# A linear-attention plus spectral-mixing kernel: f32 x is no longer kept from the attention stage but formed again during the weight stream, and nine modes of weights are prefetched instead of seven

## The chip, the cores and the metric

The kernel runs on one core of a Trainium2 chip. The metric is the device time of one execution in microseconds (us). The profile of a kernel comes from one execution; its span (first to last instruction) is about 1.8 us shorter than the time of the same execution. In the profile PE is TensorE (PEld its weight loads), DVE is VectorE, ACT is ScalarE, POOL is GpSimd and SP is SyncE. The kernel keeps its tiles in SBUF and the results of its matmuls in PSUM, two memories of the core.

## The reference, cut to what matters

```python
# attention: q, k, v are (B=8, H=8, S=576, Dh=64)
q_p, k_p = phi(q), phi(k)                       # phi(x) = elu(x) + 1
kv  = einsum('bhsd,bhse->bhde', k_p, v)         # 64 x 64 for each head
z   = sum(k_p, axis=2)
x   = einsum('bhsd,bhde->bhse', q_p, kv) / (einsum('bhsd,bhd->bhs', q_p, z) + 1e-6)
x   = x.transpose(0, 2, 1, 3).reshape(B, S, 512)
# spectral mixing: 64 modes, each with its own 512 x 512 complex weight
X = rfft(x, axis=1)[:, :64]
Yr = Xr @ w_r - Xi @ w_i ;  Yi = Xr @ w_i + Xi @ w_r      # per mode
u = x + irfft(Y, n=S, axis=1)
out = u + maximum(u @ w_ch, 0)
```

The weights w_r and w_i are 64 x 512 x 512 f32 each, 134 MB together; q, k and v are 28 MB. The kernel lets the DMA cast everything to 16 bits on the way into SBUF. One **half mode** below is w_r or w_i of one mode: 1 MB in memory, 512 KB in SBUF.

## The kernel before

The kernel has three stages. Attention runs over eight batches and produces f32 x (kept in SBUF to the end) and its transform `xt_c`. Then the weight stream multiplies mode after mode, with the products x @ w_ch of 36 tiles of x spread between the modes. The last stage transforms back, adds and writes the output.

Attention needs the transform of **all** batches before mode 0 can be multiplied, so weights that arrive during attention have to be stored. Two pools do that: `wpre` (4 buffers, used once, inside the attention scope) holds modes 0 and 1, and `wpool` (10 buffers, recycled for the whole stream) holds modes 2 to 6.

```python
x_main = [xpool.tile([128, NJJ, D], F32, ...) for b in range(B)]     # 64 KB a partition
x_tail = [xpool.tile([128, D], F32, ...) for i in range(B // 2)]     #  8 KB a partition
W_KEEP = 10                     # recycled half-mode buffers
W_PRE = 4                       # half-mode buffers used once
n_pre = W_PRE // 2

for b in range(B):
    for nm, src in (("q", q), ("k", k), ("v", v)):
        t = sA.tile([...], F16, tag="raw", bufs=5, ...)      # one ring for q, k and v
        nc.gpsimd.dma_start(out=t, in_=...)
    # ... weights for mode b/2 - 1; phi(q), phi(k); k^T v; q^T into qT (bufs=1) ...
    for jj in range(NJJ + 1):
        # num = qT^T @ [kv | z]  (8 small matmuls)
        nc.vector.reciprocal(out=rden[orow], in_=nv[:, :, :, 64])
        dst = xtl[orow, :] if tail else xm[:, jj, :]                 # f32 x, kept
        nc.vector.tensor_tensor(out=dst, in0=nv[..., 0:64], in1=rden..., op=ALU.mult)
        if tail: nc.scalar.copy(out=x16t[orow, :], in_=dst)
        else:    nc.gpsimd.tensor_copy(out=x16[:, jj, :], in_=dst)   # f16 copy for the transform
    # ... xf = transform of x16 (20 matmuls); xt_c <- xf (VectorE and ScalarE) ...

def mode_product(kk, ...):
    wr, wi = w_get(kk)          # loads a later mode into the buffers that are freed
    # P = 4 matmuls with wr, 4 with wi; P -> f16; 4 small matmuls into yt_ps
# ... modes 0..63, after mode 4 also: channel_product(t): x16w <- x_of(t), transposes, eps = xT^T @ wch, E0[t] <- eps
```

A load can only be issued when its buffer is free, and all loads of q, k, v and w are issued by POOL, in order. The engines execute their own instructions in the order that the compiler's scheduler gave them.

Of the kernel before, what the change touches and what calls it, by code (L numbers as in the profile page):

```python
# [16 lines left out]
NJ = 9  # L17
# [3 lines left out]
def _dft_consts(S: int, NM: int):  # L21
# [5 lines left out]
    for jj in range(4):  # L27
        for j2 in range(2):
            s = NJ * p + 2 * jj + j2
            ang = 2.0 * np.pi * np.outer(s, m) / S  # L30
            fwd[j2 * 64 : j2 * 64 + 64, jj, :NM] = np.cos(ang)
            fwd[j2 * 64 : j2 * 64 + 64, jj, NM:] = -np.sin(ang)
            s_cols[jj * 128 + j2 * 64 + p] = s
# [20 lines left out]
def kernel(  # L54
# [46 lines left out]
    x_main = [  # L101
        xpool.tile([128, NJJ, D], F32, tag="x_main", bufs=B, name=f"x_main{b}") for b in range(B)
    ]
    x_tail = [
        xpool.tile([128, D], F32, tag="x_tail", bufs=B // 2, name=f"x_tail{i}")
        for i in range(B // 2)
    ]
# [9 lines left out]
    W_KEEP = 10  # L117

    def w_load(kk: int, pool, tag: str, bufs: int):
        got = []  # L120
        for name, src in (("wr", moe_w_r), ("wi", moe_w_i)):
            w = pool.tile([128, NDC, D], BF16, tag=tag, bufs=bufs, name=f"{name}{kk}")
            nc.gpsimd.dma_start(out=w, in_=src[kk].rearrange("(p dc) e -> p dc e", dc=NDC))
            got.append(w)
        return got
# [4 lines left out]
    sA_ctx = ExitStack()  # L130
    sA = sA_ctx.enter_context(tc.tile_pool(name="sA", bufs=1))
    psA = sA_ctx.enter_context(tc.tile_pool(name="psA", bufs=1, space=bass.MemoryType.PSUM))
    W_PRE = 4
    wpre = sA_ctx.enter_context(tc.tile_pool(name="wpre", bufs=1))
    n_pre = W_PRE // 2

    vpad = [sA.tile([128, NHP, NJ, 66], F16, tag="vpad", bufs=1, name=f"vpad{i}") for i in range(1)]
    for t in vpad:
        nc.vector.memset(t[:, :, :, 64:66], 1.0)

    for b in range(B):
        raw = {}
        for nm, src in (("q", q), ("k", k), ("v", v)):
            t = sA.tile([128, NHP, NJ * Dh], F16, tag="raw", bufs=5, name=f"{nm}16_{b}")
            nc.gpsimd.dma_start(
                out=t,
                in_=src[b].rearrange("h s d -> (h s) d").rearrange(
                    "(hp r j) d -> r hp (j d)", r=128, j=NJ
                ),
            )  # L150
            raw[nm] = t
        if b % 2 == 0 and b > 0:
            kk = b // 2 - 1
            if kk < n_pre:
                w_in[kk] = w_load(kk, wpre, "wp", W_PRE)
            else:
                w_in[kk] = w_load(kk, wpool, "w", W_KEEP)

# [15 lines left out]
        vp = vpad[0]  # L174
# [18 lines left out]
        kv_sb = sA.tile([128, 2, 2, 65], F16, tag="kv_sb", bufs=2, name=f"kvs{b}")  # L193
# [9 lines left out]
        qT = sA.tile([128, 2, 2, NJ * NP], F16, tag="qT", bufs=1, name=f"qT{b}")  # L203
        qp = phi["q"]
        for hpp in range(2):
            qT_ps = psA.tile([128, NJ, 2, NP], F16, tag="big", bufs=3, name=f"qTp{b}_{hpp}")
            for j in range(NJ):
                nc.tensor.transpose(
                    qT_ps[:, j].rearrange("p t r -> p (t r)"),
                    qp[:, hpp, j].rearrange("p o d -> p (o d)"),  # L210
                    id16,
                )
# [5 lines left out]
        xm, xtl = x_main[b], x_tail[b // 2]  # L218
# [3 lines left out]
        for jj in range(NJJ + 1):  # L222
# [3 lines left out]
            for hpp in range(2):  # L226
                for h2 in range(2):
                    for hpo in range(2):
                        rows = slice(hpo * 64, hpo * 64 + 64)
                        c0 = (hpp * 2 + h2) * 65  # L230
                        cols = slice(512, 576) if tail else slice(jj * 128, jj * 128 + 128)
                        nc.tensor.matmul(  # L232
                            num[orow, hpo, c0 : c0 + 65],
                            qT[rows, hpp, h2, cols],
                            kv_sb[rows, hpp, h2, :],
                        )
            nv = num[orow, :, 0:260].rearrange("p o (c n) -> p o c n", c=4)
            rden = sA.tile([128, 2, 4], F32, tag="rden", bufs=3, name=f"rd{b}_{jj}")
            nc.vector.reciprocal(out=rden[orow], in_=nv[:, :, :, 64])
            dst = xtl[orow, :] if tail else xm[:, jj, :]  # L240
# [3 lines left out]
                in1=rden[orow].unsqueeze(3).broadcast_to([64 if tail else 128, 2, 4, Dh]),  # L244
                op=ALU.mult,
            )
            if tail:
                nc.scalar.copy(out=x16t[orow, :], in_=dst)
            else:
                nc.gpsimd.tensor_copy(out=x16[:, jj, :], in_=dst)  # L250
# [14 lines left out]
    n_in = len(w_in)  # L265


    def w_get(kk: int):
        if kk not in w_in:
            w_in[kk] = w_load(kk, wpool, "w", W_KEEP)  # L270
        return w_in.pop(kk)

    def mode_product(kk: int, ps, stage, yt_ps):

        wr, wi = w_get(kk)
        P = ps.tile([128, D], F32, tag="P", bufs=2, name=f"P{kk}")
# [21 lines left out]


    nc.gpsimd.dma_start(out=wch16, in_=moe_w_ch.rearrange("(c p) j -> p c j", p=128))  # L300
    while n_in < n_pre + W_KEEP // 2:
        w_in[n_in] = w_load(n_in, wpool, "w", W_KEEP)
        n_in += 1
    first = {}
    for kk in range(n_pre):
        first[kk] = w_in[kk]

    ystage0 = ctx.enter_context(tc.tile_pool(name="ystage", bufs=1, side="right"))
    def open_w_psum():
        return tc.alloc_tile_pool(name="psW", bufs=1, space=bass.MemoryType.PSUM)  # L310

    st_first = []
    for kk in range(n_pre):
        wr, wi = w_get(kk)
        P = psA.tile([128, D], F32, tag="xf", bufs=2, name=f"P{kk}")
        for t, w in ((0, wr), (1, wi)):
            for dc in range(NDC):
                quad = slice(dc * 32, dc * 32 + 32)
                nc.tensor.matmul(
                    P[quad, :], xt_cols(dc, 1 - t, kk), w[:, dc, :],  # L320
                    start=(t == 0), stop=(t == 1), tile_position=(0, dc * 32),
                )
        st = ystage0.tile([128, D], F16, tag="ystage", bufs=2, name=f"ys{kk}")
        if kk % 2 == 0:
            nc.vector.tensor_copy(out=st, in_=P)
        else:
            nc.scalar.copy(out=st, in_=P)
        st_first.append(st)
    sA_ctx.close()

    sW = ctx.enter_context(tc.tile_pool(name="sW", bufs=1))
    psW = open_w_psum()
    YT = sW.tile([128, NDC, NM, 2 * B], F16, name="YT")
    E0 = [sW.tile([128, D], F16, tag="E0", bufs=36, name=f"E0_{i}") for i in range(36)]
    YZ = [sW.tile([128, 2, D], F16, tag="YZ", bufs=B, name=f"YZ{b}") for b in range(B)]

    def x_of(t: int):
        return x_main[t // NJJ][:, t % NJJ, :] if t < B * NJJ else x_tail[t - B * NJJ]

    def channel_product(t: int):  # L340
        x16 = sW.tile([128, D], F16, tag="x16w", bufs=2, name=f"x16w{t}")
        nc.scalar.copy(out=x16, in_=x_of(t))
# [10 lines left out]
        nc.scalar.copy(out=E0[t], in_=e_ps)  # L353

    yt_ps = None
    done = 0
    for kk in range(NM):
        if kk % 8 == 0:
            yt_ps = psW.tile([128, NDC, 8, 2 * B], F32, tag="yt_ps", bufs=1, name=f"yt{kk // 8}")
        if kk < n_pre:  # L360
            for ec in range(NDC):
                nc.tensor.matmul(
                    yt_ps[:, ec, kk % 8, :], st_first[kk][:, ec * 128 : ec * 128 + 128], pick_sb
                )
        else:
            mode_product(kk, psW, ystage0, yt_ps)
        if kk % 8 == 7:
            g0 = kk - 7
            nc.vector.tensor_copy(out=YT[:, :, g0 : g0 + 8, :], in_=yt_ps)
        if 4 <= kk < 52:  # L370
            want = (kk - 3) * 36 // 48
            while done < want:
                channel_product(done)
                done += 1
        if kk == NE - 1:

            for b in range(B):
                z_ps = psW.tile([128, D], F32, tag="z_ps", bufs=1, name=f"z{b}")
                y_ps = psW.tile([128, D], F16, tag="y_ps", bufs=1, name=f"yp{b}")
                for ec in range(NDC):  # L380
                    lhs = YT[:, ec, 0:NE, :].rearrange("p m (t b) -> p (m t) b", b=B)[:, :, b]
                    nc.tensor.matmul(  # L382
                        z_ps[: 2 * NE, :], lhs, wch16[:, ec, :],
                        start=(ec == 0), stop=(ec == NDC - 1),
                    )
                for ec in range(NDC):
                    lhs = YT[:, ec, 0:NE, :].rearrange("p m (t b) -> p (m t) b", b=B)[:, :, b]
                    nc.tensor.transpose(  # L388
                        y_ps[: 2 * NE, ec * 128 : ec * 128 + 128], lhs, id16
                    )  # L390
                nc.scalar.copy(out=YZ[b][: 2 * NE, 1, :], in_=z_ps[: 2 * NE, :])
                nc.vector.tensor_copy(out=YZ[b][: 2 * NE, 0, :], in_=y_ps[: 2 * NE, :])


    last = sW.tile([128, 2, D], F16, tag="last", bufs=1, name="last")
    z_ps = psW.tile([128, D], F32, tag="z_ps", bufs=1, name="zl")
# [99 lines left out]
```

## Time and profile before

The median of four runs is 471.41 us (470.15 to 472.33). The whole-span shares of the profile hide the structure, so this table goes by stage.

| stage | from, to (us) | what limits it |
|---|---|---|
| attention, DMA busy | 1 to 111 | loads, 200 to 211 GB/s written after the first slice |
| attention, DMA idle | 111 to 134 | no free weight buffer; attention's own chain |
| weight stream | 134 to 415 | weight loads, 212 to 214 GB/s by the slice |
| tail | 417 to 469 | 8 us of last products, 33 us of VectorE, 10 us of output and end |

The page of the kernel before. The first line is busy time per engine; the two lines below it are the DMA rows of the 40 slices (each 11.7 us); the last one is the head of the chain that ended last.

```profile
PE 261.8 (56%) x2156; PEld 139.6 (30%) x2156; DVE 156.6 (33%) x288; ACT 140.9 (30%) x211; POOL 128.7 (27%) x205
...
DMA  9999999995069999999999999999999999943985
GB/s 160 207 211 208 210 203 208 209 200 102 1 122 212 214 212 213 214 214 213 214 214 214 213 213 213 213 214 214 213 213 213 214 214 214 213 82 107 285 272 166
...
DMA 63%; PE 15%; DVE 10%; ACT 6%; issue 2%; POOL 2%; POOLq 0%; ACTq 0%; SPq 0%
```

No compute engine is near full, and the DMA row is at 9 almost everywhere; the exceptions are slices 10 to 12 and the end. Those three slices are the hole. The table of stretches of the kernel before shows its edges (columns: stretch, its length, busy us and count of PE, PEld, DVE, ACT and POOL, granted TensorE clock, DMA share, GB/s):

```profile
108.00:110.00 2.00, 1.02 (x24) 0.70 (x24) 1.62 (x6) 0.00 (x0) 0.53 (x1) 0.50 1.06 213
110.00:112.00 2.00, 1.86 (x25) 1.25 (x27) 1.97 (x6) 0.00 (x0) 1.83 (x4) 0.50 0.68 135
112.00:114.00 2.00, 2.00 (x30) 1.43 (x24) 0.17 (x1) 0.62 (x1) 0.03 (x1) 0.50 0.00 0
...
130.00:132.00 2.00, 1.31 (x20) 0.81 (x20) 0.14 (x1) 1.68 (x3) 0.00 (x0) 0.50 0.00 0
132.00:134.00 2.00, 2.00 (x24) 1.01 (x17) 0.88 (x2) 0.78 (x3) 1.78 (x4) 0.50 0.34 25
134.00:136.00 2.00, 2.00 (x20) 0.62 (x15) 0.54 (x2) 0.44 (x1) 0.92 (x3) 0.61 0.91 174
```

What ends the hole is read from the timeline of the kernel before, PE first: the first mode product, then mode 2's product, whose buffer belongs to the recycled ring (start, duration, engine, line, operation).

```profile
128.29 0.68 PE L319 MATMUL P_1509<-wr_451,xt_c 128*32 128x512 bf16 x4 [1.20 <-ACT xt_c L263]
...
131.23 0.68 PE L279 MATMUL P_1594<-wr_1147,xt_c 128*32 128x512 bf16 x4
```

And POOL's timeline of the same execution, the first load after the hole. The bracket gives the idle time before it and who ended it: PE, by finishing with mode 2.

```profile
132.22 0.54 POOL L123 DMA_DIRECT2D wr_1699<-in_moe_w_r_dram  x1 [8.74 <-PE P_1594 L279]
```

So the sequence is: attention ends, modes 0 and 1 are multiplied, mode 2 is multiplied, its buffer is free, the load is issued, and traffic resumes about 1.5 us later. Nothing of this is visible in busy shares.

The weight stream ends with the last weight product, which waits for the last load (PE's timeline of the kernel before):

```profile
417.35 0.67 PE L285 MATMUL P_3387<-wi_3385,xt_c 128*32 128x512 bf16 x4 [1.83 <-DMA wi_3385<-in_moe_w_i_dram]
```

Attention's own end has a cause too. ScalarE's timeline shows a wait for a load with batch 5's work queued behind it:

```profile
92.28 1.16 ACT L167 ACTIVATE ke_1329<-k_7_1319 128x1152 f16<-128x1152 f16 x1 [7.01 <-DMA k_7_1319<-in_k_dram]
93.46 1.12 ACT L213 COPY qT_1028<-qTp_0_1029 128x1152 f16<-128x1152 f16 x1
...
105.57 1.12 ACT L213 COPY qT_1204<-qTp_0_1205 128x1152 f16<-128x1152 f16 x1 [2.62 <-PE qTp_0_1205 L208]
```

ScalarE stood 7.0 us until batch 7's k had landed, and the copies of batch 5's q^T (`qT_1028`) came only after that. The third line is batch 6's first q^T copy.

### The profile page before, as it was taken

The page shows a single profiled execution, that of the slowest core. Times are in us where ns is not written, and L with a number is a line of the kernel's source. Part 1 is how long each engine was busy: PE and PEld are TensorE (multiplying, and loading weights), DVE is VectorE, ACT ScalarE, POOL GpSimd, SP SyncE. Part 2 cuts the span into 40 slices and gives each one's busy share as a digit, 9 for nine tenths or more (in the row PEclk, how much of TensorE's full clock was granted, in tenths as well). Part 3 has the DMA queues.
Part 4 walks back from the last instruction along what each step waited for, and adds up shares of the span by engine and source line. Part 5 has one row for each costly group of instructions (what it writes and reads, how often), then busy time and mean ns, then how long its engine had stood idle before and what let it go on. Part 6 is the DMA issues. An engine that isn't in the chain of part 4 may idle for free.

```text
span 469.2 us, 5483 instructions
## 1 busy us (share of the span) xinstructions
PE 261.8 (56%) x2156; PEld 139.6 (30%) x2156; DVE 156.6 (33%) x288; ACT 140.9 (30%) x211; POOL 128.7 (27%) x205
## 2 busy tenths in 40 slices
PE   0386557678586675677675332333333379349970
PEld 0254334455333333333332110111111158113320
DVE  1686569565332112112121100100101012017991
ACT  3666567253233434344341000000000013002320
POOL 3354335332241212222222212222222212004561
PEclk9955577555678989988979555555555569657996
DMA  9999999995069999999999999999999999943985
GB/s 160 207 211 208 210 203 208 209 200 102 1 122 212 214 212 213 214 214 213 214 214 214 213 213 213 213 214 214 213 213 213 214 214 214 213 82 107 285 272 166
DMA packets 37738, 92.20 MB, mean 197 GB/s; under 512 B 3536, under 2 KB 16592, under 8 KB 37712
## 3 DMA queue, kind: packets, MB, share of 16 engines
q0 software_dynamic: 31632, 81.80, 90.0%
q1 hardware_dynamic: 3328, 5.20, 3.7%
q10 hardware_dynamic: 2752, 4.85, 3.3%
q8 instruction: 17, 0.28, 0.2%
q14 instruction: 9, 0.07, 0.0%
HBM read 163.93 MB, written 9.44 MB: 369 GB/s over the span
## 4 chain that ended last, share of the span: by engine, by line
DMA 63%; PE 15%; DVE 10%; ACT 6%; issue 2%; POOL 2%; POOLq 0%; ACTq 0%; SPq 0%
DMA wi_3385<-in_moe_w_i_dram 4%; DMA wr_2310<-in_moe_w_r_dram 4%; DMA wr_3076<-in_moe_w_r_dram 4%; DMA wr_2955<-in_moe_w_r_dram 4%; DMA wr_2832<-in_moe_w_r_dram 4%; DMA wr_2588<-in_moe_w_r_dram 4%; DMA wr_2467<-in_moe_w_r_dram 4%; DMA wr_3250<-in_moe_w_r_dram 4%; DMA wr_2711<-in_moe_w_r_dram 4%; DMA wr_2187<-in_moe_w_r_dram 4%; DMA wr_2066<-in_moe_w_r_dram 4%; DMA wr_1943<-in_moe_w_r_dram 4%; DMA wr_1822<-in_moe_w_r_dram 4%; DMA k_1_275<-in_k_dram 3%; DMA k_4_795<-in_k_dram 2%
## 5 line engine op out<-in xcount | busy, mean ns | idle before, releaser
L285 PEld LDWEIGHTS <-xt_c 128*32 128x32 bf16 x248 | 18.0, 154 | 82.0 <-issue 80.7
L279 PEld LDWEIGHTS <-xt_c 128*32 128x32 bf16 x248 | 13.7, 157 | 43.5 <-issue 17.6
L186 PE MATMUL kvp_120<-vpad_99,ke_113 64*128 64x130 f16 x36 | 2.1, 309 | 16.1 <-DVE ke_113 L172 16.1
L441 POOL TENSOR_TENSOR x_main_76<-x_main_76,r_3441 128x512 f32<-128x512 f32 x1 | 1.3, 1267 | 30.1 <-ACT r_3441 L440 30.1
L382 PEld LDWEIGHTS <-YT 128*112 128x112 f16 x32 | 7.7, 288 | 2.7 <-issue 2.2
L388 PEld LDWEIGHTS <-YT 128*112 128x112 f16 x32 | 7.4, 292 | 0.4
L186 PEld LDWEIGHTS <-ke_113 64*128 64x128 f16 x36 | 1.9, 141 | 16.1 <-DVE ke_113 L172 16.1
L424 PEld LDWEIGHTS <-inv_sb 128*128 128x128 f16 x32 | 3.3, 103 | 8.9 <-issue 7.0
L419 PEld LDWEIGHTS <-id_64 128*128 128x128 f16 x36 | 3.6, 102 | 5.7 <-issue 2.1
L423 PEld LDWEIGHTS <-inv_sb 128*128 128x128 f16 x32 | 3.3, 105 | 5.5 <-issue 2.7
L250 POOL CAST x_5_1051<-x_main_81 128x512 f16<-128x512 f32 x4 | 2.4, 622 | 9.5 <-DVE x_main_81 L241 9.5
L250 POOL CAST x_7_1399<-x_main_83 128x512 f16<-128x512 f32 x4 | 2.4, 616 | 9.1 <-DVE x_main_83 L241 9.1
L250 POOL CAST x_6_1227<-x_main_82 128x512 f16<-128x512 f32 x4 | 2.4, 618 | 7.7 <-DVE x_main_82 L241 7.7
L167 ACT ACTIVATE ke_1329<-k_7_1319 128x1152 f16<-128x1152 f16 x2 | 2.3, 1168 | 7.0 <-DMA k_7_1319<-in_k_dram 7.0
L232 PE MATMUL num_0_1053<-kvs_1025,qT_1028 64*128 64x65 f16 x8 | 0.6, 236 | 6.3 <-ACT qT_1028 L213 6.3
L167 ACT ACTIVATE qe_107<-q_0_101 128x1152 f16<-128x1152 f16 x2 | 2.2, 1154 | 5.9 <-DMA q_0_101<-in_q_dram 5.9
L291 DVE CAST ys_3377<-P_3368 128x512 f16<-128x512 f32 x1 | 0.7, 692 | 9.3 <-PE P_3368 L285 9.3
L167 ACT ACTIVATE ke_809<-k_4_795 128x1152 f16<-128x1152 f16 x2 | 2.3, 1167 | 4.9 <-DMA k_4_795<-in_k_dram 4.9
L250 POOL CAST x_2_531<-x_main_78 128x512 f16<-128x512 f32 x4 | 2.4, 618 | 4.9 <-DVE x_main_78 L241 4.9
L291 DVE CAST ys_2845<-P_2836 128x512 f16<-128x512 f32 x1 | 0.7, 692 | 9.1 <-PE P_2836 L285 9.1
L291 DVE CAST ys_2601<-P_2592 128x512 f16<-128x512 f32 x1 | 0.7, 692 | 9.1 <-PE P_2592 L285 9.1
L291 DVE CAST ys_2533<-P_2524 128x512 f16<-128x512 f32 x1 | 0.7, 692 | 9.1 <-PE P_2524 L285 9.1
(1284 smaller groups left out, 823.8 us busy)
## 6 DMA issues: line engine op xcount, KB each, us to landing
q_0_101<-in_q_dram POOLq DMA_DIRECT2D x1, 576.0 KB, 6.9
k_0_103<-in_k_dram POOLq DMA_DIRECT2D x1, 576.0 KB, 8.8
v_0_105<-in_v_dram POOLq DMA_DIRECT2D x1, 576.0 KB, 10.9
q_1_273<-in_q_dram POOLq DMA_DIRECT2D x1, 576.0 KB, 13.0
k_1_275<-in_k_dram POOLq DMA_DIRECT2D x1, 576.0 KB, 15.1
v_1_277<-in_v_dram POOLq DMA_DIRECT2D x1, 576.0 KB, 9.2
q_2_445<-in_q_dram POOLq DMA_DIRECT2D x1, 576.0 KB, 10.3
k_2_447<-in_k_dram POOLq DMA_DIRECT2D x1, 576.0 KB, 10.8
```

Source lines behind the costliest of these rows:

```text
L167: nc.scalar.activation(out=ev[:, c], in_=rv[:, c], func=AF.Exp)
L186: nc.tensor.matmul(kv_ps[:, h2, hpp * 130 : hpp * 130 + 130], kp[rows, hpp, j].rearrange("p o d -> p (o d)"), vp[rows, hpp::2, j, 0:65], s ...
L250: nc.gpsimd.tensor_copy(out=x16[:, jj, :], in_=dst)
L279: nc.tensor.matmul(P[quad, :], xt_cols(dc, 1, kk), wr[:, dc, :], start=True, stop=False, tile_position=(0, dc * 32),)
L285: nc.tensor.matmul(P[quad, :], xt_cols(dc, 0, kk), wi[:, dc, :], start=False, stop=True, tile_position=(0, dc * 32),)
L291: nc.vector.tensor_copy(out=st, in_=P)
L382: nc.tensor.matmul(z_ps[: 2 * NE, :], lhs, wch16[:, ec, :], start=(ec == 0), stop=(ec == NDC - 1),)
L388: nc.tensor.transpose(y_ps[: 2 * NE, ec * 128 : ec * 128 + 128], lhs, id16)
L419: nc.tensor.matmul(e, id16, E0[t], start=True, stop=False, skip_group_check=True)
L423: nc.tensor.matmul(y, lhs, YZ[b][:, 0, :])
L424: nc.tensor.matmul(e, lhs, YZ[b][:, 1, :], start=False, stop=True, skip_group_check=True)
L441: nc.gpsimd.tensor_tensor(out=x, in0=x, in1=r, op=ALU.add)
```

## The change

The intent is to take the 72 KB a partition of f32 x out of the attention stage and spend the room on weight buffers. Attention keeps per batch the transposed q (4.6 KB a partition), k^T v and 1/den, from which x can be formed again: 8 small matmuls and one VectorE multiply per tile. That is done in the weight stream, tile by tile, just before the tile's channel product. Nine modes are prefetched instead of seven, and the recycled ring now holds the **first** modes (0 to 3), the one-time buffers modes 4 to 8. Raw q, k and v get two buffers each, and padded v two. The POOL and ScalarE casts go, because VectorE writes f16 x straight from PSUM. Rows are ordered so that an output transfer writes 4 KB runs instead of 2 KB runs. The ReLU ring goes from 3 to 2 buffers, for room.

```diff
-            s = NJ * p + 2 * jj + j2
+            s = NJ * p + 4 * j2 + jj
...
-    x_main = [ ... F32 ... in xpool ]                  # now allocated after attention
+    q_tile = lambda name: xpool.tile([128, QW], F16, tag="qTE", bufs=B + 1, name=name)
+    kv_all = [xpool.tile([128, 2, 2, 65], F16, tag="kv", bufs=B, ...) for b in range(B)]
+    rd_all = [xpool.tile([128, 5, 2, 4], F32, tag="rd", bufs=B, ...) for b in range(B)]
-    W_KEEP = 10
+    W_KEEP = 8
-    W_PRE = 4
+    W_PRE = 10
+    def w_next():
+        kk, half = pending.pop(0)
+        pool, tag, bufs = (wpool, "w", W_KEEP) if kk < n_keep else (wpre, "wp", W_PRE)
...
-            t = sA.tile([...], F16, tag="raw", bufs=5, ...)
+            t = sA.tile([...], F16, tag=f"{nm}16", bufs=2, ...)
-        if b % 2 == 0 and b > 0:
-            ... both halves of mode b // 2 - 1 ...
+        if b >= 1:
+            w_next()
-        vp = vpad[0]
+        vp = vpad[b % 2]
...
-            dst = xtl[orow, :] if tail else xm[:, jj, :]
+            dst = x16t[orow, :] if tail else x16[:, jj, :]
             nc.vector.tensor_tensor(out=dst..., in0=nv[:, :, :, 0:64], in1=rden..., op=ALU.mult)
-            if tail:
-                nc.scalar.copy(out=x16t[orow, :], in_=dst)
-            else:
-                nc.gpsimd.tensor_copy(out=x16[:, jj, :], in_=dst)
...
     def channel_product(t: int):
+        num = psW.tile([128, 2, 512], F32, tag="num", bufs=1, name=f"nw{t}")
+        for b, jj, orow in parts:
+            nv = num_matmuls(num, orow, q_view(qT_all[b]), kv_all[b], jj)
+            nc.vector.tensor_tensor(out=x[orow, :]..., in0=nv[:, :, :, 0:64],
+                                    in1=rd_all[b][orow, jj]..., op=ALU.mult)
         nc.scalar.copy(out=x16, in_=x)
...
-                        out=ov[:, 2 * (jj - 1) + j2 : 2 * jj + j2 + 1 : 2, :],
+                        out=ov[:, 4 * j2 + jj - 1 : 4 * j2 + jj + 1, :],
-            r = sW.tile([128, D], F32, tag="relu", bufs=3, name=f"r{t}")
+            r = sW.tile([128, D], F32, tag="relu", bufs=2, name=f"r{t}")
```

Cut: a third PSUM buffer for P (two before), the multiplication of all nine prefetched modes before the first channel product, how E0 reuses the qT buffers, the formation of the last rows two batches per mode instead of all eight at once, and the tail tiles' split products.

## The prediction

> **What bounds the kernel now.** The DMA engines: the DMA row of the 40-slice view is at 9 in nearly every slice, and the chain of waits gives DMA 63%. The stretch table shows a steady 213–214 GB/s from 136 to 415 us: one 512 KB half mode per 2.45 us. The stream has one hole: traffic stops at 111.3 us, when all 14 half modes that have a buffer are loaded, and is back at about 133.7. These 22.4 us end when attention is finished (first mode product at 128.3 in the timeline) and mode 2, the first whose buffer is in the recycled ring, is multiplied (131.2; next load issued at 132.2). After the last weight (417.3) come 52 us of tail: 8 us to the first output add, 33 us of VectorE at 100%, 5 us of output transfers, 5 us of fixed end.
>
> **What the change does.**
> 1. Without f32 x in attention, 18 half modes fit instead of 14: 4 x 2.45 = 9.8 us of traffic moves into the hole, which then begins at about 121.
> 2. The ring starts with mode 0, so the first load of the stream waits for mode 0, not mode 2: about 3 us less.
> 3. Attention loses the POOL casts (32 x 0.6 us) and the ScalarE tail casts, since VectorE writes f16 from PSUM; 1.5–2 us of the last batch's chain. By the instruction order batch 7's k is queued behind 9 half modes instead of 7, so it lands at about 98–100 (92.3 before), but its exp now comes after batch 5's q^T copies, not before. Before, batch 6's first q^T copy (105.6) to the first mode product took 22.7 us; after, that copy starts near 102.5, so the first product at about 123 (121–126).
> 4. Added in the stream: 36 tiles x (8 small matmuls, 0.3–0.4 us, and one VectorE multiply, 0.66 us). PE is busy 54 of 100 us and VectorE 15 of 100 there: free. The ring has 8 halves instead of 10; issue to landing took 19.1 us, so 8 were in flight already: no cost. Nine early modes at 1.5–2 us take 13–18 us, while the four modes loaded meanwhile take 19.6: no second hole, but little margin.
> 5. Tail: same VectorE steps. Output rows become 4 KB runs instead of 2 KB; the Trainium skill ("Perfetto Trace Analysis", DMA Optimizations) says such batching helps, but VectorE sets this stage: at most 1 us.
>
> **Sum.** Traffic back at 123 + 2.5 = 125.5 against an end of prefetch at 121: a hole of 4–5 us instead of 22.4, about 18 us less. Bytes and rates of the stream are unchanged. 471.8 - 18 = 454 us, range 447 to 460. Faster by over 2%: 0.92; within 2%: 0.07; slower: 0.01.
>
> **What would show it.** Hole between 120 and 127, under 8 us; first mode product at 121–126; last weight near 399–400; from there to the end still 51–52 us; stream at 213–214 GB/s with no hole near 140–150; PE busier by 10–20 us, POOL less by about 20.
>
> **What would make it wrong.** The first product comes no earlier than 128 (late k of batch 7, PE at half clock): only 13 us won. POOL's in-order queue of loads waits for a q or k buffer and starves the DMA before 121. The early modes exceed 20 us and open a second hole. The added PE, VectorE and PSUM steps (one numerator buffer) delay consumption beyond the ring's slack. If the hole closes fully, 450.

## The result, and the profile after

The changed kernel takes 454.16 us (453.89 to 454.59, four runs) against 471.41 us. The ratio of the two is 0.9637 with a 95% interval of 0.9611 to 0.9662. Ratios here are the mean time of one kernel's runs over that of the other's in the same rounds, so they are not quite the ratio of the medians quoted. Executions over 1.5% slower than the fastest of the same kernel are left out of the means.

The same lines of the page for the changed kernel (a slice is now 11.3 us):

```profile
PE 270.5 (60%) x2488; PEld 147.4 (33%) x2488; DVE 181.2 (40%) x329; ACT 136.8 (30%) x207; POOL 107.9 (24%) x173
...
DMA  9999999999689999999999999999999999925884
GB/s 156 211 209 209 208 207 210 210 213 214 126 164 213 214 214 213 212 214 214 214 214 214 212 214 214 214 214 213 214 212 214 214 213 214 213 48 173 271 263 147
...
DMA 64%; PE 15%; DVE 11%; ACT 4%; issue 2%; POOL 1%; POOLq 0%; DVEq 0%; ACTq 0%; SPq 0%
```

The three weak slices of before have become two partly filled ones (126 and 164 GB/s). VectorE is 24.6 us busier and PE 8.7 us, POOL 20.8 us less. The stretches around the hole of the changed kernel, the same columns:

```profile
118.00:120.00 2.00, 1.31 (x12) 0.64 (x11) 1.93 (x7) 0.00 (x0) 0.00 (x0) 0.50 0.90 182
120.00:122.00 2.00, 1.53 (x10) 0.92 (x10) 0.41 (x1) 0.00 (x0) 0.00 (x0) 0.50 0.16 31
122.00:124.00 2.00, 1.08 (x7) 0.57 (x6) 0.69 (x1) 0.15 (x1) 0.00 (x0) 0.50 0.00 0
124.00:126.00 2.00, 1.72 (x16) 0.80 (x20) 0.49 (x1) 0.23 (x1) 0.53 (x1) 0.50 0.00 0
126.00:128.00 2.00, 2.00 (x21) 0.69 (x13) 0.26 (x2) 0.58 (x1) 1.59 (x3) 0.50 0.67 90
...
140.00:150.00 10.00, 8.87 (x85) 4.25 (x85) 4.49 (x9) 3.61 (x7) 2.64 (x5) 0.81 1.06 214
```

The traffic missing between 104 and 140 us, expressed as time at 213 GB/s, is 23.0 us before and 7.2 us after (36 us less the sum of the 2 us stretches' GB/s x 2 / 213). That is 15.8 us of the 16.4 us by which the two profiled spans differ. The 140 to 150 stretch shows that no second hole opened.

The releasers, first PE's timeline, then POOL's, of the changed kernel:

```profile
124.28 0.68 PE L279 MATMUL P_1442<-wr_274,xt_c 128*32 128x512 bf16 x4 [1.20 <-ACT xt_c L265]
```

```profile
125.27 0.53 POOL L121 DMA_DIRECT2D wr_1603<-in_moe_w_r_dram  x1 [22.42 <-PE P_1442 L279]
```

The first mode product comes at 124.3 us instead of 128.3, and the first load is released by that product itself, 1.0 us later; before, it was issued 3.9 us after the first product. In ScalarE's timeline of the changed kernel, batch 7's loads are still waited for, but batch 5's copies are no longer behind them:

```profile
89.96 1.12 ACT L231 COPY qT_980<-qTp_1_992 128x1152 f16<-128x1152 f16 x1
94.33 2.22 ACT L183 ACTIVATE qe_1254<-q_7_1246 128x1152 f16<-128x1152 f16 x2 [3.25 <-DMA q_7_1246<-in_q_dram]
99.60 2.22 ACT L183 ACTIVATE ke_1260<-k_7_1248 128x1152 f16<-128x1152 f16 x2 [3.06 <-DMA k_7_1248<-in_k_dram]
...
102.77 1.11 ACT L231 COPY qT_1143<-qTp_0_1144 128x1152 f16<-128x1152 f16 x1
```

PE's timeline of the changed kernel has the last weight product here:

```profile
400.38 0.67 PE L285 MATMUL P_3689<-wi_3687,xt_c 128*32 128x512 bf16 x4 [1.82 <-DMA wi_3687<-in_moe_w_i_dram]
```

The last weight product (P, the w_i half of mode 63) starts at 417.35 us before and at 400.38 us after. From there to the end of the span it is 51.9 us before and 52.4 us after. So the weight stream ends 17.0 us earlier, and the tail gives 0.6 us of that back.

### The profile page after: what moved, and what is told of

It is laid out like the page before. It is cut to its first block, busy times and chain, and to the rows that moved or that the text cites. A ratio compares the mean times of both kernels' runs of the same rounds, so it can differ in the third digit from the quotient of the medians.

```text
span 452.8 us, 6147 instructions
## 1 busy us (share of the span) xinstructions
PE 270.5 (60%) x2488; PEld 147.4 (33%) x2488; DVE 181.2 (40%) x329; ACT 136.8 (30%) x207; POOL 107.9 (24%) x173
## 4 chain that ended last, share of the span: by engine, by line
DMA 64%; PE 15%; DVE 11%; ACT 4%; issue 2%; POOL 1%; POOLq 0%; DVEq 0%; ACTq 0%; SPq 0%
DMA wr_3038<-in_moe_w_r_dram 4%; DMA wi_2350<-in_moe_w_i_dram 4%; DMA k_7_1248<-in_k_dram 4%; DMA wi_2161<-in_moe_w_i_dram 4%; DMA wi_2009<-in_moe_w_i_dram 4%; DMA wr_2697<-in_moe_w_r_dram 4%; DMA wr_2861<-in_moe_w_r_dram 4%; DMA wr_3378<-in_moe_w_r_dram 4%; DMA wr_2546<-in_moe_w_r_dram 4%; DMA wr_3202<-in_moe_w_r_dram 4%; DMA wr_3480<-in_moe_w_r_dram 4%; DMA wi_1856<-in_moe_w_i_dram 4%; DMA wi_3687<-in_moe_w_i_dram 4%; DMA v_4_761<-in_v_dram 4%; DMA q_2_431<-in_q_dram 3%; DMA v_0_111<-in_v_dram 2%
## 5 line engine op out<-in xcount | busy, mean ns | idle before, releaser
L285 PEld LDWEIGHTS <-xt_c 128*32 128x32 bf16 x256 | 18.2, 156 | 70.5 <-issue 68.8
L279 PEld LDWEIGHTS <-xt_c 128*32 128x32 bf16 x256 | 15.4, 156 | 39.2 <-issue 21.8
L152 PEld LDWEIGHTS <-qT_328 64*128 64x128 f16 (+1 forms) x80 | 2.6, 111 | 12.1 <-DVE x_1_351 L247 8.2
L152 PEld LDWEIGHTS <-qT_165 64*128 64x128 f16 (+1 forms) x80 | 2.4, 120 | 7.5 <-ACT qT_165 L231 4.4
L291 DVE CAST ys_2962<-P_2953 128x512 f16<-128x512 f32 x1 | 0.7, 692 | 10.1 <-PE P_2953 L285 10.1
L152 PEld LDWEIGHTS <-qT_980 64*128 64x128 f16 (+1 forms) x80 | 2.5, 101 | 6.5 <-issue 3.4
L291 DVE CAST ys_3679<-P_3670 128x512 f16<-128x512 f32 x1 | 0.7, 690 | 9.3 <-PE P_3670 L285 9.3
L291 DVE CAST ys_3391<-P_3382 128x512 f16<-128x512 f32 x1 | 0.7, 691 | 9.2 <-PE P_3382 L285 9.2
L291 DVE CAST ys_2809<-P_2800 128x512 f16<-128x512 f32 x1 | 0.7, 692 | 9.2 <-PE P_2800 L285 9.2
L291 DVE CAST ys_3051<-P_3042 128x512 f16<-128x512 f32 x1 | 0.7, 692 | 9.2 <-PE P_3042 L285 9.2
L291 DVE CAST ys_3429<-P_3420 128x512 f16<-128x512 f32 x1 | 0.7, 692 | 9.1 <-PE P_3420 L285 9.1
## 6 DMA issues: line engine op xcount, KB each, us to landing
k_2_433<-in_k_dram POOLq DMA_DIRECT2D x1, 576.0 KB, 13.3
```

What stands on the lines that cost most here:

```text
L152: nc.tensor.matmul(num[orow, hpo, c0 : c0 + 65], qT[rows, hpp, h2, cols], kv_sb[rows, hpp, h2, :])
L279: nc.tensor.matmul(P[quad, :], xt_cols(dc, 1, kk), wr[:, dc, :], start=True, stop=False, tile_position=(0, dc * 32),)
L285: nc.tensor.matmul(P[quad, :], xt_cols(dc, 0, kk), wi[:, dc, :], start=False, stop=True, tile_position=(0, dc * 32),)
L291: nc.vector.tensor_copy(out=st, in_=P)
```

## The experiments

All variants are edits of the changed kernel, except the last. All were correct. They ran on other occasions than the change (the kernel before took 471.05, 471.72 and 471.24 us beside them, 471.41 us beside the change), so a difference of less than about 1 us between a variant and the change is not taken as shown. The first product scatters too: it came at 123.4 us (rows2k), 124.3 us (the change) and 124.5 us (twice), though the sources of these three differ in the attention only in the order of rows. A variant's own releases and stretches are read in the same way as above. The main theory is the one of the prediction: the time of this kernel is the DMA's traffic plus the hole, and the hole lasts from the filling of the last weight buffer to the release of the first.

### 1. Seven modes prefetched again (label pre6)

```diff
-    W_PRE = 10
+    W_PRE = 6
```

> Seven modes prefetched as before, all else of the change kept. If the filled hole is what counts (main theory): traffic stops 4 half modes sooner, near 110.5 us instead of 120.3, comes back at the same 127 us, and the time rises by 4 x 2.45 = 9.8 us to about 464 (463 to 465). If the gain came mainly from the shorter attention chain (rival), the time stays under 457.

Measured: 463.63 us (463.36 to 464.89), which is 9.5 us more than the change. Traffic stops at about 110 us instead of 120.5, the first product comes at 124.1 us, and the first load of the stream is issued at 125.1 us. The stretches and POOL's timeline of this variant:

```profile
108.00:110.00 2.00, 2.00 (x27) 1.40 (x23) 0.81 (x3) 0.00 (x0) 0.00 (x0) 0.50 0.94 188
110.00:112.00 2.00, 2.00 (x20) 1.27 (x20) 0.01 (x1) 0.00 (x0) 0.00 (x0) 0.50 0.12 23
```

```profile
125.08 0.53 POOL L121 DMA_DIRECT2D wr<-in_moe_w_r_dram  x1 [33.00 <-PE P L279]
```

The hole's end did not move, its start did, and the time followed one for one. The four extra half modes are worth 9.5 us.

### 2. The ring holds the last prefetched modes, as before (label ringlast)

```diff
-        pool, tag, bufs = (wpool, "w", W_KEEP) if kk < n_keep else (wpre, "wp", W_PRE)
+        pool, tag, bufs = (wpre, "wp", W_PRE) if kk < n_pre else (wpool, "w", W_KEEP)
```

> Nine modes prefetched, but modes 0 to 4 sit in the one-time buffers and modes 5 to 8 in the recycled ones, so the first load of the stream waits for mode 5. Main theory (the first release ends the hole): mode 5 is multiplied 6.2 us after mode 0, so the hole is 6.2 us longer and the time about 460.4 (459.5 to 461.5). Rival (which mode holds the ring does not matter, the prefetched count does): 454.

Measured: 459.63 us (459.36 to 460.08), 5.5 us more than the change. The first product comes at 123.6 us, but the first load is issued only at 129.6 us, when mode 5 has been multiplied. PE's timeline, then POOL's:

```profile
123.59 0.68 PE L279 MATMUL P<-wr,xt_c 128*32 128x512 bf16 x4 [1.20 <-ACT xt_c L265]
```

```profile
129.62 0.53 POOL L121 DMA_DIRECT2D wr<-in_moe_w_r_dram  x1 [27.46 <-PE P L285]
```

Which mode sits in the recycled buffers is a term of its own. Here the load comes 6.0 us after the first product, against 1.0 us in the change: 5.0 us for five modes by the trace, 5.5 us by the time. In the kernel before it cost two modes, 2.9 us by the trace (128.29 to 131.23).

### 3. Ten modes prefetched (label pre12)

```diff
-    W_PRE = 10
+    W_PRE = 12
```

> Ten modes prefetched instead of nine. Main theory: 2 x 2.45 = 4.9 us more of the remaining hole is filled (6.5 us to about 1.6), time about 449.3 (448.5 to 450.5). Rival (the hole is no longer what limits after nine modes): 454.

Measured: 449.39 us (449.16 to 449.55), 4.8 us less than the change and 0.9537 of before (0.9519 to 0.9555). Two more half modes take 4.9 us at 2.45 us each, so the relation is still one to one. The stretches of this variant show what is left of the hole:

```profile
124.00:126.00 2.00, 2.00 (x21) 0.70 (x13) 0.69 (x1) 0.21 (x1) 1.06 (x2) 0.50 0.51 84
126.00:128.00 2.00, 2.00 (x25) 0.79 (x20) 0.69 (x1) 0.37 (x1) 1.26 (x3) 0.76 0.78 135
```

Two more would not fit: the allocator refused 14 one-time buffers when the kernel was built.

### 4. x formed twice in the stream (label twice)

```diff
-        for b, jj, orow in parts:
+        for b, jj, orow in parts + parts:
```

> The forming of f32 x in the stream is done twice (the same result written again): about 15 us more PE work and 24 us more VectorE work in the stream. Main theory (free in the shadow of the weight loads): 454.2, within 0.7 us. Rival (the added work delays the release of weight buffers): 2 us or more slower.

Measured: 455.46 us (454.42 to 455.75). This is 1.3 us above the change's median, more than the 0.7 us expected, though below the 2 us of the rival; the two kernels ran on different occasions and the intervals of their ratios to before overlap (0.9643 to 0.9682, 0.9611 to 0.9662). PE rose from 270.5 to 311.6 us and VectorE from 181.2 to 207.0 us, while traffic stayed at 213 to 214 GB/s from 140 to 380 us. About 15 us more of PE had been expected; the profiled execution also had a lower mean granted clock (0.685, against 0.734 for the change), and the trace does not separate the two. So 41 us of PE and 26 us of VectorE cost 1.3 us at most, and the two profiled spans differ by 0.6 us (453.4 and 452.8). Forming x once in the stream is free or nearly so; whether these tenths are real stays open.

### 5. A third buffer for raw k (label k3)

```diff
-            t = sA.tile([...], F16, tag=f"{nm}16", bufs=2, ...)
+            t = sA.tile([...], F16, tag=f"{nm}16", bufs=3 if nm == "k" else 2, ...)
```

> A third buffer for raw k, nothing else by hand; the compiled order then puts batch 7's k behind 7 half modes instead of 9 and q behind 7. Theory A (attention's end is set by when batch 7's q and k land, 99.6 us for k): k lands near 85, the first mode product comes at 119 to 121 instead of 124.3 and the time falls to 450.5 to 452.5. Theory B (attention's end is set by its own chain of PE, ScalarE and VectorE work at half PE clock, the load only happens to be waited for): first product still at 123 to 124.5, time 453.5 to 454.5.

Measured: 454.23 us (453.62 to 454.70): no gain. The first product comes at 123.2 us. Both are what theory B said, and this would speak for it. But ScalarE's timeline of this variant shows why not to stop here:

```profile
93.93 2.22 ACT L183 ACTIVATE qe<-q 128x1152 f16<-128x1152 f16 x2 [2.63 <-DMA q<-in_q_dram]
96.05 2.20 ACT L183 ACTIVATE ke<-k 128x1152 f16<-128x1152 f16 x2
```

In the compiled order k is behind 6 half modes, one fewer than the expectation states, and its wait is gone, as intended. But q is still waited for until 93.9 us, as in the change (94.3). And VectorE's first step on batch 7's q stands in its order **ahead** of the last product of batch 5, which the transform of batch 5 needs. From VectorE's timeline of the changed kernel:

```profile
96.58 0.76 DVE L184 TENSOR_SCALAR q_7_1246<-q_7_1246 128x2304 f16<-128x2304 f16 x1 [1.96 <-ACT qe_1254 L183]
97.37 0.69 DVE L247 TENSOR_TENSOR x16t_1004<-num_4_1049,rd_91 64x512 f16<-64x512 f32 x1
```

Batch 5's tail product waited 2.0 us for batch 7's q, with which it has nothing to do: its own reciprocal had been done at 94.62 us (`rd_91`, start 94.41 us, 0.21 us long). That gave theory C: two loads hold the attention's end, q through VectorE's order and k through ScalarE's, and freeing one leaves the other.

### 6. A third buffer for raw q (label q3)

```diff
+            ... bufs=3 if nm == "q" else 2 ...
```

> A third buffer for raw q only; the compiled order puts batch 7's q behind 6 half modes, k stays behind 9. Theory C (two loads hold attention's end in turn: VectorE waits for q's exp ahead of batch 5's tail product, then ScalarE waits for k; freeing one leaves the other): k still lands near 99.5, first product within 1.2 us of 124.3, time 453.3 to 454.7. If q alone held it: first product near 121.5, time 451.5.

Measured: 453.77, 454.61 and 454.85 us in three executions, so again no gain, as theory C expects (if q alone held the end, 451.5 us had been expected). The fourth execution, which was the profiled one, took 627.19 us, with no reading of the granted clock below 1.0 and yet matmuls that took twice as long (985 ns in the mean for one with w_ch, 435 ns in k3); its cause is not known, and its trace is not used. So where k landed in this variant is not read from a trace, and that k was what held the end here is inferred from the next experiment.

### 7. Third buffers for raw q and raw k (label qk3)

```diff
-    vpad = [... tag="vpad", bufs=2 ... for i in range(2)]      # room for the two buffers
+    vpad = [... tag="vpad", bufs=1 ... for i in range(1)]
-            t = sA.tile([...], F16, tag=f"{nm}16", bufs=2, ...)
+            t = sA.tile([...], F16, tag=f"{nm}16", bufs=2 if nm == "v" else 3, ...)
```

> Third buffers for raw q and raw k (one padded v tile to make room); batch 7's q and k both come behind 6 half modes and land before 92. Theory C: VectorE's 2 us wait and ScalarE's 3 us waits both go, first product near 121.5 (120.5 to 122.3), time 451 to 452.5. Theory B (PE, ScalarE and VectorE work alone sets attention's end): first product 123 to 124.5, time 453.5 to 454.7.

Measured: 449.06 us (448.25 to 449.15), 5.1 us less than the change and 0.9529 of before (0.9514 to 0.9544). The time is below the 451 to 452.5 us expected: theory C is confirmed in kind and was too careful in size. ScalarE's timeline of this variant:

```profile
84.31 2.22 ACT L183 ACTIVATE qe<-q 128x1152 f16<-128x1152 f16 x2 [0.30 <-DMA q<-in_q_dram]
87.11 2.22 ACT L183 ACTIVATE ke<-k 128x1152 f16<-128x1152 f16 x2 [0.59 <-DMA k<-in_k_dram]
```

The first product comes at 118.5 us, and the stretches of this variant show traffic nearly without a break:

```profile
118.00:120.00 2.00, 1.50 (x16) 0.78 (x20) 0.30 (x2) 0.38 (x1) 0.50 (x1) 0.50 0.91 182
120.00:122.00 2.00, 2.00 (x21) 0.51 (x9) 0.42 (x1) 0.59 (x1) 1.61 (x4) 0.50 0.66 88
122.00:124.00 2.00, 2.00 (x36) 1.12 (x36) 0.85 (x2) 0.59 (x1) 1.49 (x3) 0.98 1.02 205
```

Neither buffer alone moved the time; both together moved it by 5 us. The single padded v tile is not what did it: experiment 11 has it too, with k's buffer alone, and its first product comes at 123.7 us. In all these variants the compiled order of the loads moved with the buffers, so what is shown is the effect of the two places in the order, not of the buffers as such. The chain of waits of this variant leads from batch 7's v to the first product; the wait is that of VectorE's copy of v, which is now behind 8 half modes (6 in the change):

```profile
97.49 0.76 DVE L191 COPY vpad<-v 128x2304 f16<-128x2304 f16 x1 [4.23 <-DMA v<-in_v_dram]
```

### 8. The casts back in (label cast)

```diff
-            dst = x16t[orow, :] if tail else x16[:, jj, :]
+            xs = sA.tile([128, D], F32, tag="xs", bufs=3, ...)
+            dst = xs[orow, :]
             nc.vector.tensor_tensor(out=dst..., ...)
+            if tail: nc.scalar.copy(out=x16t[orow, :], in_=dst)
+            else:    nc.gpsimd.tensor_copy(out=x16[:, jj, :], in_=dst)
```

> The attention writes f32 x to a scratch tile again and POOL (ScalarE for the tail) casts it to f16, as before; prefetch and ring as in the change. The compiled order of loads also moves (batch 7's k behind 7 halves), which can't be held. Main theory: the casts cost 1.5 to 2 us of the last batch's chain, first product near 126, time 455 to 456.5. Rival (casts and the loads queued behind them were the larger part of the gain): 458 or more. If the earlier k outweighs them: 453.

Measured: 454.49 us (454.32 to 455.00), no slower beyond the noise; the first product comes at 123.9 us. This run does not separate its two effects. From batch 6's first q^T copy to batch 7's first it takes 12.7 us here and 11.2 us in the change, 1.5 us more, and from batch 6's first copy to the first product 24.2 us against 21.5 us. This is what longer chains by the casts would look like, but the compiled order is not the same in the two kernels. The scheduler put batch 7's k ahead of three half modes and w_ch (it is behind 6 halves, not the 7 that the expectation states), batch 6's copies started at 99.7 us instead of 102.8, and the sum is a first product at 123.9 us instead of 124.3. What the casts alone are worth is therefore not shown.

### 9. The old buffers of q, k and v (label oldbufs)

```diff
-            t = sA.tile([...], F16, tag=f"{nm}16", bufs=2, ...)
+            t = sA.tile([...], F16, tag="raw", bufs=5, ...)
-    vpad ... bufs=2 ... range(2)
+    vpad ... bufs=1 ... range(1)
```

> Shared ring of five raw buffers and one padded v tile, as before the change, all else of the change kept. The compiled order puts batch 7's v behind about 13 half modes, by the bytes landing near 108 us. Main theory (buffers only matter through batch 7's landing): first product 125 to 127, time 455 to 457. Rival 1 (own buffers made attention shorter by the whole 4 us): first product at 128 or later, time 458 or more. Rival 2 (no effect): 454.

Measured: 460.66 us (460.58 to 460.69), 6.5 us more than the change, with the first product at 130.3 us. Batch 7's v landed at 109.3 us, as expected from the bytes ahead of it, but the expectation of 125 to 127 us for the first product was wrong: the copy of v stands in VectorE's order before all of batch 6's products, so 21 us of work followed it and not 16. Own buffers for q, k and v are a necessary part of the change, because with weights interleaved they decide how far back batch 7 is queued.

### 10. Output rows as 2 KB runs (label rows2k)

```diff
-            s = NJ * p + 4 * j2 + jj
+            s = NJ * p + 2 * jj + j2
-                j = 8 if sl == 8 else 4 * (sl % 2) + sl // 2
+                j = sl
-                        out=ov[:, 4 * j2 + jj - 1 : 4 * j2 + jj + 1, :],
+                        out=ov[:, 2 * (jj - 1) + j2 : 2 * jj + j2 + 1 : 2, :],
```

> Output rows as 2 KB runs again, all else of the change kept. Main theory (VectorE at 100% sets the last stage): time 454.2 within 0.7 us; last weight to end 52 us either way. Rival (4 KB runs speed the output transfers): 1 us or more slower.

Measured: 454.83 us (454.59 to 455.43), 0.7 us above the change's median and 0.6 above k3's, which ran on the same chip in the same rounds. That is at the edge of what was expected. VectorE's last add ends at 441.2 us and the last output transfer is issued 2.0 us after it; in the change 1.1 us after. From the last weight product to the end it takes 53.2 us here, and 52.3 to 52.9 us in the variants with 4 KB runs. So the longer runs may save about half a microsecond, at the very end.

### 11. Ten modes and a third buffer for raw k (label p12k3)

```diff
-    W_PRE = 10
+    W_PRE = 12
+            ... bufs=3 if nm == "k" else 2 ...       (and one padded v tile)
```

> Ten modes prefetched and a third buffer for raw k (one padded v tile to make room): both helps together. Main theory: only about 1.7 us of hole was left at ten modes, so 448 to 449.4; nothing below 447.3, the time with no hole at all. If the first product comes later because of the single padded v tile, up to 450.5.

Measured: 449.33 us (448.96 to 449.56), the same as ten modes alone (449.39). The first product is at 123.7 us in both. q is still waited for until 94.3 us, so k alone changed nothing, as in experiment 5. Ten modes with third buffers for both q and k does not fit either (seen when building), so the two ways to close the hole were not combined. Both end near 449 us because both leave at most 2.0 us of missing traffic.

### 12. The kernel before, with two ReLU buffers (label b_relu2)

```diff
-            r = sW.tile([128, D], F32, tag="relu", bufs=3, name=f"r{t}")
+            r = sW.tile([128, D], F32, tag="relu", bufs=2, name=f"r{t}")
```

> The kernel before with two ReLU buffers instead of three, as the change has them. If the shorter ring is what lets the last output transfers be issued 1 us or more after the last VectorE add (0.2 us in the kernel before, 1.1 in the changed one): the gap rises to about 1 us and the time by 0.5 to 1 us, to about 472. If not: the gap stays near 0.2 us, time as before.

Measured: 474.05 us (471.91 to 476.90) against 471.24 us, ratio 1.0067 (1.0020 to 1.0115). That is more than the 0.5 to 1 us expected. VectorE's last add of this variant, and then its last output issue on SP:

```profile
458.99 0.69 DVE L443 SCALAR_TENSOR_TENSOR x_tail<-e,x_tail 128x512 f32<-128x512 f32 x1
```

```profile
461.48 1.17 SPq L461 DMA_DIRECT2D out_dram<-x_tail  x1
```

The gap is 1.8 us, where the kernel before has 0.2 us (459.61 to 459.82). With two buffers POOL's adds run in pairs of 2.5 us, and the last pair is late: it ends at 460.8 us, 1.1 us after VectorE's last add. In this trace the last weight product comes at 416.11 us, so the tail takes 54.8 us instead of 51.9. The smaller ReLU ring can thus lengthen the tail. That it is what the tail of the change loses is likely and not shown, because the change was not run with three buffers, and its loss of 0.6 us is much smaller. The size in time is uncertain also because the executions of this variant scatter more than those of the others.

## Why the prediction was right, point by point

One check covers all kept traces. The third column is the measure used above: the traffic missing between 104 and 140 us, as time at 213 GB/s.

| run | span, us | missing traffic, us | span less missing traffic, us |
|---|---|---|---|
| before | 469.2 | 23.0 | 446.2 |
| the change | 452.8 | 7.2 | 445.6 |
| pre6 | 462.1 | 16.9 | 445.2 |
| ringlast | 457.7 | 11.7 | 446.0 |
| pre12 | 447.6 | 2.0 | 445.6 |
| twice | 453.4 | 7.5 | 445.9 |
| k3 | 452.3 | 6.3 | 446.0 |
| qk3 | 447.3 | 1.4 | 445.9 |
| cast | 452.5 | 6.7 | 445.8 |
| oldbufs | 458.8 | 13.3 | 445.5 |
| rows2k | 452.8 | 6.4 | 446.4 |
| p12k3 | 447.5 | 1.6 | 445.9 |
| b_relu2 | 470.9 | 22.0 | 448.9 |

The spans differ by up to 22 us, and without the hole twelve of the thirteen agree within 1.2 us. The exception is b_relu2, whose tail is 2.9 us longer.

- **What bounds the kernel.** Right. Every variant that moved the hole's start or its end moved the time nearly one for one (experiments 1, 2, 3, 7 and 9), and doubling the compute that was added in the stream moved it by 1.3 us at most (4).
- **Four more half modes.** Predicted 9.8 us, measured 9.5 us by undoing it. The hole began near 120.5 us; 121 was predicted.
- **The ring starts with mode 0.** Predicted 3 us. The trace shows 2.9 us between the first product and mode 2's before, and undoing it for five modes cost 5.5 us.
- **Attention ends earlier.** First product predicted at about 123 us, measured at 124.3 us. The steps: k of batch 7 at 98 to 100 us (measured 99.6), batch 6's first copy near 102.5 (102.8), then 22.7 us less 1.5 to 2 us (measured 21.5 us, so only 1.2 us less). The place of the number was right, but its causes were only partly right. What the missing casts gave is not shown (8), and the buffers of q, k and v, which the prediction does not mention, are indispensable (9). The new end was moved by when batch 7's q and k land, through the order of two engines' queues (5, 6, 7).
- **Added work is free.** Essentially right: 213 to 214 GB/s from 140 us on, no second hole. PE rose by 8.7 us, less than the 10 to 20 predicted; VectorE by 24.6 us and POOL by -20.8 us, as predicted.
- **Tail.** Predicted 51 to 52 us, measured 52.4 us, just above. The 4 KB runs gave at most about half a microsecond, within the "at most 1 us". That a smaller ReLU ring can cost time was not foreseen (12).
- **Sum.** About 18 us was predicted for the hole, 15.8 us was measured between the traces. The stream ends 17.0 us earlier, and the remaining 1.2 us comes from fuller traffic earlier: from the start to 104 us the kernel before moved 202 GB/s and the changed one 204, worth about 1.0 us, most of it between 100 and 104 us (178 and 215 GB/s). The hole is 6 to 7 us long, not 4 to 5, mainly because the first product came 1.3 us later than predicted; with the scatter given above (123.4 to 124.5 us) part of that is chance. The predicted 454 us thus agrees with 454.16 us to 0.2 us partly by luck: the hole gave 2.2 us less than predicted and the tail lost 0.6 us, while the earlier traffic gave 1.2 us more, the medians lie 0.9 us further apart than the two profiled executions (17.3 against 16.4 us), and the median before is 0.4 us below the 471.8 us that the prediction started from.

Left open: whether the doubled work's 1.3 us is real, what the casts alone are worth, the size in time of the ReLU ring in the changed kernel, and what a version with ten modes, early q and k and three ReLU buffers would give.

## What to carry to other kernels

In a kernel bound by loads, look for the stretches in which no load runs, and read each one as two instants: when the last free buffer was filled, and what frees the first one. More buffers move the first instant, a better choice of **which** data sits in the recycled buffers moves the second, and both were worth nearly their full length here; so is the work that has to end before the first release. When a wait is removed and nothing improves, look in the order of the in-order engines for a second wait that ends at nearly the same time: here two changes worth nothing alone were worth 5 us together.

## What the Trainium skill lacked or had wrong

- "DMA: Bandwidth & Descriptors", Where 436 GB/s comes from: its warning says that for transfers between HBM and SBUF the HBM side (about 358 GB/s) binds, and does not say in words that a core running alone is not held to it. With one core running, as here, the kernel reads f32 weights at about 427 GB/s throughout the stream (213 to 214 GB/s written as bf16, from twice as many bytes). This agrees with that page's own single-core measurement of 425 GB/s for 16 MB. The page's bandwidth tables do not say by which side a casting load is to be counted; here 512 KB in SBUF took 2.45 us, which is 1 MB at 428 GB/s on the side that is read. A load without a cast was not run beside it.
- The same page, Queues, rings and completion order: it does not mention how many loads are in flight before the issuing engine waits. Here POOL's issues wait for the completion of an earlier load (for instance 2.31 us for batch 7's k before a weight load at 99.86 us); in the changed kernel each weight load from 84.29 to 102.32 us waits for the load issued eight places before it, and a load that is issued behind a full queue lands about 19 us later: k of batch 7 was issued at 80.46 us and landed at 99.6. The traces do not show which part of the system sets that limit. It makes the place in the queue of loads as important as the time of issue.
- "Perfetto Trace Analysis", DMA Optimizations: it says that batching from 2 KB to 4 KB "can dramatically improve throughput", and calls this the primary optimization when a kernel is DMA-bound. The runs do not contradict it, they show a stage outside that condition: where VectorE limits the stage, the time was 454.83 us with 2 KB runs against 454.16 (the change) and 454.23 us (k3, same rounds) with 4 KB runs.
- "Perfetto Trace Analysis", Identifying Dependency Chains, speaks of the semaphores that an instruction waits for. That ScalarE, VectorE and GpSimd take their instructions in strict order stands elsewhere on the page (Tensor Engine Instruction); what is lacking is the consequence, that an instruction waiting for one batch's load delays ready work of another batch behind it on the same engine. Here batch 5's product stood 2.0 us behind batch 7's q, and moving both loads forward was worth 5.1 us, each alone nothing.
